# Copies of bank A ahead of norm and halves in the steps of a block pair; the norm by two chunks; weight work spread over four places

## The chip, the cores and the metric

One core of one Trainium2 chip. The metric is the device time of the whole program in microseconds (us). TensorE (PE) multiplies, PEld are its weight loads; ScalarE is ACT, VectorE is DVE, GpSimd is POOL, and SyncE, SP, issues most transfers.

## The reference, cut to what matters

```python
kv = np.einsum('bhsd,bhse->bhde', k, v)           # 8 batches, 8 heads, 576 tokens, 64 per head
out = np.einsum('bhsd,bhde->bhse', q, kv)
rms = np.sqrt(np.mean(out * out, axis=-1, keepdims=True) + 1e-06)
x = out / rms * g_norm                            # then to 4608 tokens x 512
gate = 1.0 / (1.0 + np.exp(-(x @ w_gate)))        # w_gate, w_val: 512 x 1536
x = gate * (x @ w_val) @ w_out                    # w_out: 1536 x 512
h = x @ w_in                                      # 512 x 2048
g = np.where(h >= 1, h, np.where(h <= -1, 0.0, (h + 1) ** 2 / 4))
return g @ w_out2                                 # 2048 x 512
```

## The kernel before, in words

The 4608 tokens are nine blocks of 512, transposed: rows are channels, columns tokens. A number in fp32 is kept as two fp32r halves (`split`: ScalarE copies the high half, VectorE subtracts for the low one), and a product of two such numbers is three matmuls. Blocks 0 and 1 run first while the weights arrive, then blocks 2, 3 and 4 one at a time: for each of twelve slices f of the hidden layer 24 matmuls for gate and value, then `down`, 12 matmuls that add the slice's share to four accumulator banks. Blocks 5 and 6 are the first block pair, blocks 7 and 8 the second and last. After them class `Second` computes the second layer for all blocks; it is not touched.

A pair takes gate and value of two blocks together by a scheme of seven products (names a11, a12, a22, s1, s2, s3, s4; L648, six matmuls each) in place of eight. Bank A collects a11, then s2, s1 and s4 on top of it; between them ScalarE must copy it away: to bank D (pD), to u2, to u4, and at last through the sigmoid gate2. Bank A is one buffer, so each of these stands in front of the next product on A. D gives the sigmoid `gate`. Product a22 of a step is done by `finish` in the next step, and there VectorE completes `u2`, whose halves (gh, gl) are what `down` multiplies. Bank F, the attention's X, the norm's sums SS and kvps take turns in two more banks.

Beside the steps runs other work, put at places by hand: `at(n)` in `Pair.step` calls what the plan holds for step f and place n, and `work(dve, act)` goes on with the second layer's weights (decode, sums, halves, stores), so many pieces of VectorE and ScalarE. While the first pair runs, the attention and the norm of blocks 7 and 8 are made, eight chunks of 128 channels; blocks 2 to 4 carry the norm of the blocks behind them in the same way, with places 0, 1 and 2. A chunk's norm: its square, the halves of the square, a sum over each head by matmuls with ones (SS), the mean m, a reciprocal root r (an ACT function whose table must be loaded, as the sigmoid's must be after it), one Newton step t, and two products on VectorE. `manual_schedule` leaves every engine's instructions in the order of the code.

In the last pair the down weights wo are streamed ahead (`stream(n)`: until n sets of two tiles are held), from a pool of twelve tiles that the halves of the second layer's weights (w2half) use too; a half waits for the landing of the store that used its tile before.

Of the kernel before, what the change touches and what calls it, by code (L numbers as in the profile page):

```python
# [11 lines left out]
ALU = mybir.AluOpType  # L12
# [21 lines left out]
def attn_gated_mlp_kernel(ctx: ExitStack, tc: tile.TileContext, a: dict, out: bass.AP):  # L34
# [170 lines left out]
    def norm_stage(j, p, n):  # L205

        if n == 0:
            if p % 2 == 0:
                attn_two(j, p // 2)
                for i in range(2):  # L210
                    if p == 0:
                        load_q(j, 2 + i)
                    elif j >= J0 and not is_second(j):
                        load_q(j + 1, i)
                for c in range(p, p + 2):
                    x_of(j)[c] = x_tile(j, c)
                    act_copy(x_of(j)[c], xps.pop((j, c)))
            sq = state[j, p] = temp("sq", "sq")
            nc.scalar.activation(out=sq, in_=x_of(j)[p], func=AF.Square)
        elif n == 1:  # L220
            state[j, p] = split(state[j, p], half_tile(tp, "sqh", "sqh"), half_tile(tp, "sql", "sql"))
        elif n == 2:
            SS = at_tile("SS")
            for i in range(2):
                nc.tensor.matmul(SS, ones, state[j, p][i], start=i == 0, stop=i == 1)  # L225
            m = state[j, p] = temp("m", "nm")
            nc.scalar.activation(out=m, in_=SS, func=AF.Copy, scale=1.0 / D, bias=EPS)
        elif n == 3:
            m, r, t = state[j, p], temp("r", "nr"), temp("t", "nt")
            nc.scalar.activation(out=r, in_=m, func=AF.Abs_reciprocal_sqrt)  # L230
            nc.scalar.activation(out=t, in_=r, func=AF.Square)
            nc.vector.tensor_tensor(out=t, in0=t, in1=m, op=ALU.mult)
            state[j, p] = r, t
        else:
            r, t = state.pop((j, p))
            x = x_of(j)[p]
            nc.scalar.activation(out=t, in_=t, func=AF.Copy, scale=-0.5, bias=1.5)
            nc.vector.scalar_tensor_tensor(out=x, in0=x, scalar=gn, in1=r, op0=ALU.mult, op1=ALU.mult)
            nc.vector.tensor_tensor(out=x, in0=x, in1=t, op=ALU.mult)

    def norm_plan(chunks, every):

        plan = {}
        for i, (j, p) in enumerate(chunks):
            f = every * i
            for n, place in enumerate(((f, 2), (f + 1, 0), (f + 1, 1), (f + 1, 2), (f + 2, 1))):
                plan.setdefault(place, []).append((j, p, n))
        for place in plan.values():
            place.sort(key=lambda x: x[2] if x[2] else 9)
        return plan  # L250
# [349 lines left out]
    class Pair:  # L600
# [66 lines left out]
        def step(self, side, j, f, at, more):  # L667
# [16 lines left out]
            if f:  # L684
                split_g(j, f - 1, self.finish(f - 1))
            else:
                F = bank(side, 2, "pF")
                self.product(F, f, "s3")
            at(0)
            self.product(A, f, "s2", False)  # L690
            u2 = saved(A, "u2", "wol", 2)
            at(1)
            work(*portion)
            self.product(D, f, "a12", False)
            gate = sigmoid(D, "gate")
            at(2)
            work(*portion)
            self.product(A, f, "s1", False)
            u4 = saved(A, "u4", "sig", 1)
            if f:  # L700
# [3 lines left out]
            at(3)  # L704
# [5 lines left out]
            if f == F1 - 1:  # L710
                split_g(j + 1, 0, self.g2[0])
            if f:
                down(j, f - 1)
            self.pending = F, u2, gate
            work(3, 0)
# [301 lines left out]
    with tc.manual_schedule():  # L1017
# [294 lines left out]
        chunks = lambda *js: [(j, p) for j in js for p in range(NP)]  # L1312
# [11 lines left out]
        for j in range(2, J0):  # L1324
            tail = j == J0 - 1
            plan = norm_plan(chunks(j + 1, j + 2), 1) if tail else norm_plan(chunks(j + 1), 2)

            def at(f, n):
                for which in plan.get((f, n), ()):
                    norm_stage(*which)  # L1330
# [178 lines left out]
```

## Time and profile before

| | us |
|---|---|
| median of 3 runs | 1690.81 (1690.69 to 1692.56) |
| the profiled execution | 1693.95 |
| its span | 1692.0 |
| TensorE busy, of the span | 1650.2 (98%) |
| weight loads | 1375.3 (81%) |
| VectorE busy | 1133.7 (67%) |
| ScalarE busy | 913.7 (54%) |
| GpSimd busy | 186.5 (11%) |

The shares are of the whole span. Its stages: blocks 0 and 1 to about 245 us, blocks 2 to 4 to 573, the first pair's steps to 770, the rest of that pair's `down` to 807, the second pair's steps to 958, the rest of its `down` to 998, the second layer to the end. The busy time of TensorE contains matmuls at a lower clock; the granted clock stands beside it in the windows.

### The profile page before, as it was taken

The numbers are of one execution on the slowest core, as the hardware profiler recorded it, in microseconds if no ns is written. First come the engines' busy times: TensorE is split into PE (matmuls) and PEld (weight loads), VectorE is DVE, ScalarE is ACT, GpSimd is POOL, SyncE is SP. The second block draws the span as 40 slices with busy tenths as digits, with TensorE's granted clock in tenths as the row PEclk, the third lists the DMA queues.
The fourth block names the chain that finished last, engine by engine and source line by source line (L and its number), as shares of the span: only waits on it lengthen the run. The fifth ranks groups of instructions, "written<-read, shape, count | busy, mean of one in ns | idle before, by whom it ended". The sixth has DMA issues, their size and how long they took to land.

```text
span 1692.0 us, 22526 instructions
## 1 busy us (share of the span) xinstructions
PE 1650.2 (98%) x8132; PEld 1375.3 (81%) x8132; DVE 1133.7 (67%) x1682; ACT 913.7 (54%) x1366; POOL 186.5 (11%) x292
## 2 busy tenths in 40 slices
PE   8999999999999988889999999999999999999999
PEld 6778888888877766668787778888888888999998
DVE  5888846768845755447456655894697579569476
ACT  4444445546558646544343446754664675575573
POOL 1122132332301110110211200000000000000000
PEclk8999999999999998889999999999999999999999
DMA  9676785678768575656896577556755856687855
GB/s 290 240 243 227 246 289 191 212 235 269 236 199 267 177 264 170 214 190 248 307 338 239 174 275 274 203 199 245 234 193 186 299 175 220 245 296 258 315 183 193
DMA packets 134479, 400.05 MB, mean 236 GB/s; under 512 B 16856, under 2 KB 24152, under 8 KB 120288
## 3 DMA queue, kind: packets, MB, share of 16 engines
q1 hardware_dynamic: 113440, 331.48, 58.9%
q0 software_dynamic: 20928, 67.13, 10.6%
q8 instruction: 65, 1.06, 0.3%
q14 instruction: 46, 0.38, 0.1%
HBM read 315.18 MB, written 83.36 MB: 236 GB/s over the span
## 4 chain that ended last, share of the span: by engine, by line
PE 77%; issue 13%; POOL 3%; ACT 3%; DVE 2%; DMA 2%; SPq 0%; POOLq 0%; DVEq 0%; ACTq 0%
PE bank L798 20%; PE bank L958 20%; PE pA L648 6%; PE acc L94 4%; PE acc L96 4%; PE acc L95 4%; PE h L94 4%; PE h L95 4%; PE h L96 4%; PE pF L648 3%; POOL w1d L535 1%; PE kvps L159 1%; PE X L186 1%; PE pD L648 1%; PE SS L225 1%
## 5 line engine op out<-in xcount | busy, mean ns | idle before, releaser
L958 PE MATMUL bank<-gh,wo 128*128 128x512 f32 (+1 forms) x1680 | 345.8, 367 | 0.0
L958 PEld LDWEIGHTS bank<-gh,wo 128*128 128x128 f32 x1680 | 305.7, 188 | 39.3
L69 ACT ACTIVATE gh<-g 128x1024 fp32r<-128x1024 f32 (+2 forms) x164 | 151.0, 924 | 129.6 <-PE bank L958 99.3
L798 PE MATMUL bank<-x_t,wst 128*128 128x512 f32 (+1 forms) x960 | 210.0, 367 | 0.0
L798 PEld LDWEIGHTS bank<-x_t,wst 128*128 128x128 f32 x960 | 175.1, 188 | 22.5
L648 PE MATMUL pA<-xc,wc 128*128 128x512 f32 x576 | 156.2, 408 | 29.6 <-ACT u L69 28.3
L733 DVE TENSOR_TENSOR gh<-g,gh 128x1024 fp32r<-128x1024 f32 (+1 forms) x140 | 155.9, 1114 | 29.7 <-ACT gh L69 29.4
L94 PE MATMUL acc<-gh,woh 128*128 128x512 f32 x420 | 164.9, 393 | 0.0
L95 PE MATMUL acc<-gl,woh 128*128 128x512 f32 x420 | 164.2, 391 | 0.1
L798 PE MATMUL bank<-x_b,wst 128*128 128x512 f32 (+1 forms) x720 | 160.8, 367 | 0.0
L648 PEld LDWEIGHTS pA<-xc,wc 128*128 128x128 f32 x576 | 109.2, 194 | 63.5 <-ACT u L69 39.3
L69 ACT ACTIVATE kept<-bank 128x512 f32<-128x512 f32 (+1 forms) x200 | 109.3, 549 | 95.2 <-PE bank L798 82.0
L733 DVE TENSOR_TENSOR g<-bank,kept 128x512 f32<-128x512 f32 (+1 forms) x160 | 98.1, 634 | 84.4 <-ACT kept L69 45.8
L94 PE MATMUL h<-xh,w 128*128 128x512 f32 x384 | 151.6, 395 | 0.0
L95 PE MATMUL h<-xl,w 128*128 128x512 f32 x384 | 149.8, 390 | 0.2 <-DVE xl L84 0.2
L96 PE MATMUL h<-xh,w 128*128 128x512 f32 x384 | 149.5, 389 | 0.0
L798 PEld LDWEIGHTS bank<-x_b,wst 128*128 128x128 f32 x720 | 131.5, 188 | 16.9
L96 PE MATMUL acc<-gh,woh 128*128 128x512 f32 x324 | 126.8, 391 | 1.5 <-DMA woh<-wo1d 1.5
L848 DVE SCALAR_TENSOR_TENSOR g<-r,g 128x1024 f32<-128x1024 f32 (+1 forms) x70 | 78.0, 1115 | 73.1 <-ACT r L845 73.1
L842 ACT ACTIVATE r<-g,half 128x1024 f32<-128x1024 f32 (+1 forms) x70 | 74.4, 1063 | 65.3 <-DVE g L733 65.3
L95 PEld LDWEIGHTS acc<-gl,woh 128*128 128x128 f32 x420 | 79.1, 188 | 17.2 <-DVE gl L77 0.9
L94 PEld LDWEIGHTS acc<-gh,woh 128*128 128x128 f32 x420 | 79.1, 188 | 17.2 <-issue 0.4
(191 smaller groups left out, 2573.3 us busy)
## 6 DMA issues: line engine op xcount, KB each, us to landing
wo<-wo2d SPq DMA_DIRECT2D x70, 1024.0 KB, 4.9
wc<-w1d SPq DMA_DIRECT2D x168, 256.0 KB, 5.0
woh<-wo1d SPq DMA_DIRECT2D x162, 256.0 KB, 4.9
wst<-w2d SPq DMA_DIRECT2D x40, 1024.0 KB, 5.1
wst<-w2d SPq DMA_DIRECT2D x40, 768.0 KB, 4.6
raw<-in_w SPq DMA_DIRECT2D x32, 512.0 KB, 5.3
raw<-in_w_gv SPq DMA_DIRECT2D x24, 512.0 KB, 5.7
w1d<-w2half POOLq DMA_DIRECT2D x48, 256.0 KB, 3.6
```

The costliest lines, as they stand in the source:

```text
L69: nc.scalar.activation(out=o, in_=i, func=AF.Copy)
L94: nc.tensor.matmul(ps, w[0][:, wsl], x[0], start=first, stop=False)
L95: nc.tensor.matmul(ps, w[0][:, wsl], x[1], start=False, stop=False)
L96: nc.tensor.matmul(ps, w[1][:, wsl], x[0], start=False, stop=last)
L159: nc.tensor.matmul(ps[g * D:(g + 1) * D, e], k[:, s], v[:, s], start=c == 0, stop=c == NSC)
L186: nc.tensor.matmul(X[g][e * D:(e + 1) * D, t0:t1], kvw[b % NKV][s, i, e], q[e][s, t0:t1], start=True, stop=True)
L648: nc.tensor.matmul(o, w[:, h, sl], x[c][l], start=first and c == n == 0, stop=c == 1 and n == 2, skip_group_check=True)
L733: nc.vector.tensor_tensor(out=o, in0=x, in1=y, op=op)
L798: nc.tensor.matmul(bank, self.ws[w][h][:, sl], self.xo[x][:, l, c], start=first and c == n == 0, stop=c == 1 and n == 2, skip_group_check= ...
L842: nc.scalar.activation(out=r, in_=v, func=AF.Relu, bias=self.half, scale=0.5)
L848: nc.vector.scalar_tensor_tensor(out=v, in0=r, scalar=1.0, in1=v, op0=ALU.min, op1=ALU.max)
L958: nc.tensor.matmul(bank[i][o], self.wo2[2 * i + k // 2][:, k % 2 * 2 + e, h, o * P:(o + 1) * P], ops[m][:, l, e], start=first, stop=k == H ...
```

## The change

In `Pair.step` the copy u2 is issued before the halves of the former step's result (`split_g`), u4 before the sigmoid `gate`, and `work` is called at places 1, 2 and 3 and at the end, where it takes a ScalarE piece too. Place 3 now lies behind s4 and gate2. The norm is planned by units of two chunks in eight stages: attention and the X copies, square, halves, sums, both roots side by side, both squares of the roots, the rest. The second chunk's mean, root and t take the buffers of square and halves (tags sq, sqh, sql). In the last pair at most three sets of wo are held from step 7 on, where there were five, and `finish` of the last step comes before the second layer's first loads.

```diff
--- before.py
+++ after.py
@@ -202,51 +202,71 @@
         nc.vector.tensor_tensor(out=lo, in0=sq, in1=hi.bitcast(F32), op=ALU.subtract)
         state[j, p] = hi, lo
 
-    def norm_stage(j, p, n):
-
-        if n == 0:
-            if p % 2 == 0:
-                attn_two(j, p // 2)
-                for i in range(2):
-                    if p == 0:
-                        load_q(j, 2 + i)
-                    elif j >= J0 and not is_second(j):
-                        load_q(j + 1, i)
-                for c in range(p, p + 2):
-                    x_of(j)[c] = x_tile(j, c)
-                    act_copy(x_of(j)[c], xps.pop((j, c)))
+    def norm_stage(j, i, n):
+
+        ps = 2 * i, 2 * i + 1
+        tags = ("nm", "nr", "nt"), ("sq", "sqh", "sql")
+
+        def square(p):
             sq = state[j, p] = temp("sq", "sq")
             nc.scalar.activation(out=sq, in_=x_of(j)[p], func=AF.Square)
+
+        def halves(p):
+            state[j, p] = split(state[j, p], half_tile(tp, "sqh", "sqh"), half_tile(tp, "sql", "sql"))
+
+        def mean(e):
+            SS = at_tile("SS")
+            for h in range(2):
+                nc.tensor.matmul(SS, ones, state[j, ps[e]][h], start=h == 0, stop=h == 1)
+            m = state[j, ps[e]] = temp("m", tags[e][0])
+            nc.scalar.activation(out=m, in_=SS, func=AF.Copy, scale=1.0 / D, bias=EPS)
+
+        if n == 0:
+            attn_two(j, i)
+            for e in range(2):
+                if i == 0:
+                    load_q(j, 2 + e)
+                elif j >= J0 and not is_second(j):
+                    load_q(j + 1, e)
+            for p in ps:
+                x_of(j)[p] = x_tile(j, p)
+                act_copy(x_of(j)[p], xps.pop((j, p)))
         elif n == 1:
-            state[j, p] = split(state[j, p], half_tile(tp, "sqh", "sqh"), half_tile(tp, "sql", "sql"))
+            square(ps[0])
         elif n == 2:
-            SS = at_tile("SS")
-            for i in range(2):
-                nc.tensor.matmul(SS, ones, state[j, p][i], start=i == 0, stop=i == 1)
-            m = state[j, p] = temp("m", "nm")
-            nc.scalar.activation(out=m, in_=SS, func=AF.Copy, scale=1.0 / D, bias=EPS)
+            halves(ps[0])
+            square(ps[1])
         elif n == 3:
-            m, r, t = state[j, p], temp("r", "nr"), temp("t", "nt")
-            nc.scalar.activation(out=r, in_=m, func=AF.Abs_reciprocal_sqrt)
-            nc.scalar.activation(out=t, in_=r, func=AF.Square)
-            nc.vector.tensor_tensor(out=t, in0=t, in1=m, op=ALU.mult)
-            state[j, p] = r, t
+            mean(0)
+            halves(ps[1])
+        elif n == 4:
+            mean(1)
+        elif n == 5:
+            for e, p in enumerate(ps):
+                m, r = state[j, p], temp("r", tags[e][1])
+                nc.scalar.activation(out=r, in_=m, func=AF.Abs_reciprocal_sqrt)
+                state[j, p] = m, r
+        elif n == 6:
+            for e, p in enumerate(ps):
+                m, r = state[j, p]
+                t = temp("t", tags[e][2])
+                nc.scalar.activation(out=t, in_=r, func=AF.Square)
+                nc.vector.tensor_tensor(out=t, in0=t, in1=m, op=ALU.mult)
+                state[j, p] = r, t
         else:
-            r, t = state.pop((j, p))
-            x = x_of(j)[p]
-            nc.scalar.activation(out=t, in_=t, func=AF.Copy, scale=-0.5, bias=1.5)
-            nc.vector.scalar_tensor_tensor(out=x, in0=x, scalar=gn, in1=r, op0=ALU.mult, op1=ALU.mult)
-            nc.vector.tensor_tensor(out=x, in0=x, in1=t, op=ALU.mult)
-
-    def norm_plan(chunks, every):
+            for p in ps:
+                r, t = state.pop((j, p))
+                x = x_of(j)[p]
+                nc.scalar.activation(out=t, in_=t, func=AF.Copy, scale=-0.5, bias=1.5)
+                nc.vector.scalar_tensor_tensor(out=x, in0=x, scalar=gn, in1=r, op0=ALU.mult, op1=ALU.mult)
+                nc.vector.tensor_tensor(out=x, in0=x, in1=t, op=ALU.mult)
+
+    def norm_plan(units, begin, places):
 
         plan = {}
-        for i, (j, p) in enumerate(chunks):
-            f = every * i
-            for n, place in enumerate(((f, 2), (f + 1, 0), (f + 1, 1), (f + 1, 2), (f + 2, 1))):
-                plan.setdefault(place, []).append((j, p, n))
-        for place in plan.values():
-            place.sort(key=lambda x: x[2] if x[2] else 9)
+        for k, unit in enumerate(units):
+            for n, (f, place) in enumerate(places):
+                plan.setdefault((begin(k) + f, place), []).append((norm_stage, *unit, n))
         return plan
 
     def inv_rms(SS, m, r):
...
@@ -682,26 +702,26 @@
             self.product(A, f, "a11")
             act_copy(D, A)
             if f:
-                split_g(j, f - 1, self.finish(f - 1))
+                g = self.finish(f - 1)
             else:
                 F = bank(side, 2, "pF")
                 self.product(F, f, "s3")
             at(0)
             self.product(A, f, "s2", False)
             u2 = saved(A, "u2", "wol", 2)
+            if f:
+                split_g(j, f - 1, g)
             at(1)
             work(*portion)
             self.product(D, f, "a12", False)
-            gate = sigmoid(D, "gate")
-            at(2)
-            work(*portion)
             self.product(A, f, "s1", False)
             u4 = saved(A, "u4", "sig", 1)
+            gate = sigmoid(D, "gate")
             if f:
                 F = bank(side, 2, "pF")
                 self.product(F, f, "s3")
             tt(u4, F, u4, ALU.add)
-            at(3)
+            at(2)
             work(*portion)
             self.product(A, f, "s4", False)
             gate2 = sigmoid(A, "gate2")
@@ -709,10 +729,12 @@
             tt(g2, gate2, u4, ALU.mult)
             if f == F1 - 1:
                 split_g(j + 1, 0, self.g2[0])
+            at(3)
+            work(*portion)
             if f:
                 down(j, f - 1)
             self.pending = F, u2, gate
-            work(3, 0)
+            work(3, 1)
 
 
     class Second:
...
@@ -1323,11 +1345,13 @@
 
         for j in range(2, J0):
             tail = j == J0 - 1
-            plan = norm_plan(chunks(j + 1, j + 2), 1) if tail else norm_plan(chunks(j + 1), 2)
+            every = 2 if tail else 4
+            places = (0, 2), (0, 2), (1, 0), (1, 1), (1, 2), (2, 0), (2, 1), (2, 2)
+            plan = norm_plan(units(j + 1, j + 2) if tail else units(j + 1), lambda k: every * k, places)
 
             def at(f, n):
                 for which in plan.get((f, n), ()):
-                    norm_stage(*which)
+                    which[0](*which[1:])
 
             norm_tags = ("nm", "nr", "nt", "sq")
             for f in range(F1):
...
@@ -1391,17 +1415,14 @@
             pair.g2 = {}
             plan = {}
             if more:
-                for i, (u, p) in enumerate(chunks(j + 2, j + 3)):
-                    for n, place in enumerate(((i + 1, 1), (i + 2, 0), (i + 2, 3), (i + 3, 0), (i + 3, 2))):
-                        plan.setdefault(place, []).append((norm_stage, u, p, n))
-                for place in plan.values():
-                    place.sort(key=lambda x: x[3])
+                places = (0, 1), (0, 2), (0, 3), (1, 0), (1, 2), (1, 3), (2, 0), (2, 2)
+                plan = norm_plan(units(j + 2, j + 3), lambda k: 2 * k + 1, places)
                 for u in range(2):
                     b = ((j + 3 + u) * T - 1) // S
                     if b > kv_done[0]:
                         kv_done[0] = b
                         for i in range(2):
-                            plan.setdefault((4 * u + 2 * i, 3), []).insert(0, (kv_product, b, i))
+                            plan.setdefault((4 * u + 2 * i, 2), []).insert(0, (kv_product, b, i))
                             for p in range(2 * i, 2 * i + 2):
                                 plan.setdefault((4 * u + i - 1, 3), []).append((load_kv, b, p))
 
...
@@ -1417,15 +1438,15 @@
                     n = f + F1 - 7
                     kept_wo[n] = stream_wo(n, [half_tile(tp, "wok", t, bufs=2 if t == "qraw" else 1) for t in LAST[n]])
                     wos.pop(n)
-                stream(2 if f < 7 else 4 if more else 5)
+                stream(2 if f < 7 else 4 if more else 3)
                 pair.step(side, j, f, at, more)
             acc_side[0] = side
             stream(4)
+            g = pair.finish(F1 - 1)
             if not more:
                 combos.close()
                 second = Second()
                 second.begin()
-            g = pair.finish(F1 - 1)
             down(j + 1, 0)
             split_g(j, F1 - 1, g)
             split_g(j + 1, 1, pair.g2[1])
```

What this moves on ScalarE in step 5 of the first pair, behind pD and gh (before; u_6573 is u2, u_6617 is u4):

```order
L69 ACTIVATE sqh<-sq 128x512
L230 ACT_TABLE_LOAD
L230 ACTIVATE r<-m 128x512
L231 ACTIVATE t<-r 128x512
L69 ACTIVATE u_6573<-pA 128x512
L69 ACTIVATE xn<-X 128x512 x2
L219 ACTIVATE sq<-xn 128x512
L476 ACTIVATE dt<-raw 128x512
L672 ACT_TABLE_LOAD
L672 ACTIVATE gate<-pD 128x512
L237 ACTIVATE t<-t 128x512
L69 ACTIVATE u_6617<-pA 128x512
```

The same step of the change, from the copy pD on (u_6589 is u2, u_6630 is u4):

```order
L69 ACTIVATE pD<-pA 128x512
L253 ACTIVATE t<-r 128x512 x2
L69 ACTIVATE u_6589<-pA 128x512
L69 ACTIVATE gh<-u_6465 128x512
L69 ACTIVATE xn<-X 128x512 x2
L69 ACTIVATE w2half<-dt 128x256
L69 ACTIVATE u_6630<-pA 128x512
L692 ACT_TABLE_LOAD
L692 ACTIVATE gate<-pD 128x512
L260 ACTIVATE t<-t 128x512 x2
L212 ACTIVATE sq<-xn 128x512
L69 ACTIVATE w2half<-dt 128x512
```

Before, a half of the square, a table load, a root and its square stand ahead of u2, and a table load and a sigmoid ahead of u4. Now two squares stand ahead of u2; gh, the X copies and one weight half stand between u2 and u4, and the one table load of the step follows u4. In the whole program ACT_TABLE_LOAD stands 52 times before and 28 times in the change.

ScalarE at the boundary of steps 5 and 6, from the sigmoid gate2 on, before (u_6713 is u2 of step 6):

```order
L672 ACTIVATE gate_6646<-pA 128x512
L69 ACTIVATE pD<-pA 128x512
L69 ACTIVATE gh<-u_6573 128x512
L69 ACTIVATE sqh<-sq 128x512
L230 ACT_TABLE_LOAD
L230 ACTIVATE r<-m 128x512
L231 ACTIVATE t<-r 128x512
L69 ACTIVATE u_6713<-pA 128x512
```

and in the change (u_6747 is u2 of step 6):

```order
L692 ACTIVATE gate_6667<-pA 128x512
L69 ACTIVATE sqh<-sq 128x512
L212 ACTIVATE sq<-xn 128x512
L69 ACTIVATE w2half<-su 128x512 x2
L69 ACTIVATE pD<-pA 128x512
L222 ACTIVATE m<-SS 128x512
L69 ACTIVATE sqh<-sq 128x512
L69 ACTIVATE u_6747<-pA 128x512
```

The half of the square that stood ahead of u2 now stands behind gate2, with the second chunk's square and two weight halves, and all of these are ahead of the next step's pD; behind pD come a mean and the second half.

In block 2, ScalarE from the X copies of block 3's second two chunks to a root, before:

```order
L69 ACTIVATE xn<-X 128x512 x2
L219 ACTIVATE sq<-xn 128x512
L69 ACTIVATE sqh<-sq 128x512
L69 ACTIVATE w2half<-su 128x512
L567 ACTIVATE sig<-h_3183 128x512
L227 ACTIVATE m<-SS 128x512
L69 ACTIVATE gh<-gf 128x512
L69 ACTIVATE w2half<-su 128x512
L230 ACT_TABLE_LOAD
L230 ACTIVATE r<-m 128x512
L231 ACTIVATE t<-r 128x512
```

and in the change:

```order
L69 ACTIVATE xn<-X 128x512 x2
L212 ACTIVATE sq<-xn 128x512
L69 ACTIVATE sqh<-sq 128x512
L212 ACTIVATE sq<-xn 128x512
L69 ACTIVATE w2half<-su 128x512
L587 ACTIVATE sig<-h_3185 128x512
L222 ACTIVATE m<-SS 128x512
L69 ACTIVATE sqh<-sq 128x512
L69 ACTIVATE gh<-gf 128x512
L69 ACTIVATE w2half<-su 128x512
L222 ACTIVATE m<-SS 128x512
L247 ACT_TABLE_LOAD
```

Before, a chunk has its square, its sum and its root in one go, and the next one begins two steps later. Now both chunks' squares stand together, and the second mean, which follows the second sum, stands three rows behind the half of its square.

## Rows read from the trace of the kernel before

**Rows 1.** Windows: us, busy us (instructions) by engine, TensorE's clock, DMA share, GB/s
```profile
245.00:573.00 328.00, 328.00 (x1732) 266.21 (x1731) 225.22 (x397) 200.55 (x314) 74.11 (x108) 1.00 0.69 225
573.30:770.05 196.75, 171.20 (x776) 132.54 (x775) 102.52 (x172) 105.01 (x170) 23.61 (x36) 0.93 0.61 200
595.00:613.00 18.00, 17.14 (x109) 13.70 (x108) 11.38 (x21) 6.14 (x11) 0.73 (x1) 1.00 0.96 340
807.00:958.10 151.10, 146.62 (x632) 117.05 (x631) 86.53 (x150) 57.37 (x104) 29.06 (x44) 1.00 0.75 261
```

**Rows 2.** Waits of TensorE, 573 to 770 us: total, times, longest
```profile
PE pA L648 <- ACT u L69: 24.5, 11, 3.1
PE pA L648 <- ACT gate L672: 0.7, 1, 0.7
```

**Rows 3.** Timeline of TensorE, step 3: start, us, instruction [idle before]
```profile
612.96 1.52 PE L648 MATMUL pA<-xc,wc 128*128 128x512 f32 x6
614.32 1.52 PE L648 MATMUL pF<-xc,wc 128*128 128x512 f32 x6
...
617.13 1.10 PE L186 MATMUL X<-qraw,kvw 64*64 64x448 f32 x16
618.16 1.66 PE L648 MATMUL pD<-xc,wc 128*128 128x512 f32 x6
621.63 1.67 PE L648 MATMUL pA<-xc,wc 128*128 128x512 f32 x6 [1.80 <-ACT u L69]
...
626.86 1.66 PE L648 MATMUL pA<-xc,wc 128*128 128x512 f32 x6 [1.75 <-ACT u L69]
...
631.08 1.30 PE L648 MATMUL pA<-xc,wc 128*128 128x512 f32 x5
```

**Rows 4.** Timeline of ScalarE in the same step
```profile
614.58 0.58 ACT L69 ACTIVATE pD<-pA 128x512 f32<-128x512 f32 x1 [3.55 <-PE pA L648]
617.34 0.63 ACT L69 ACTIVATE gh<-u 128x512 fp32r<-128x512 f32 x1 [2.17 <-DVE u L664]
...
618.50 1.28 ACT L230 ACT_TABLE_LOAD   x1
619.80 0.63 ACT L230 ACTIVATE r<-m 128x512 f32<-128x512 f32 x1
...
620.99 0.58 ACT L69 ACTIVATE u<-pA 128x512 f32<-128x512 f32 x1
...
623.60 1.28 ACT L672 ACT_TABLE_LOAD   x1
...
626.22 0.59 ACT L69 ACTIVATE u<-pA 128x512 f32<-128x512 f32 x1
```

**Rows 5.** The chain that ended last, step 0: start, us
```profile
580.26 1.32 PE kvps L159 x40
```

**Rows 6.** Groups by line, ScalarE: busy us, mean ns, idle before
```profile
L230 ACT ACT_TABLE_LOAD x24 | 30.8, 1283 | 0.4
```

**Rows 7.** Timeline of VectorE in the same step 3
```profile
615.88 0.69 DVE L663 TENSOR_TENSOR u<-pF,u 128x512 f32<-128x512 f32 x1 [3.00 <-PE pF L648]
...
624.23 0.75 DVE L238 SCALAR_TENSOR_TENSOR xn<-xn,gn,r 128x512 f32<-128x512 f32 x1
```

**Rows 8.** Timeline of TensorE, a step of the second pair
```profile
871.09 1.52 PE L648 MATMUL pD<-xc,wc 128*128 128x512 f32 x6
872.55 1.65 PE L648 MATMUL pA<-xc,wc 128*128 128x512 f32 x6
874.04 1.52 PE L648 MATMUL pF<-xc,wc 128*128 128x512 f32 x6
```

**Rows 9.** Waits of TensorE, 770 to 960 us
```profile
PE pA L648 <- ACT u L69: 3.8, 3, 1.7
```

**Rows 10.** Waits of ScalarE, 807 to 960 us
```profile
ACT w2half L69 <- DMA w2d<-w2half: 4.8, 2, 2.6
```

**Rows 11.** Waits, 955 us to the end
```profile
PE acc L96 <- DMA woh<-wo1d: 1.5, 3, 0.5
```

More of the change, by code (lines that the diff above doesn't have):

```diff
@@ L1311, in attn_gated_mlp_kernel @@
         pair = Pair()
-        chunks = lambda *js: [(j, p) for j in js for p in range(NP)]
+        units = lambda *js: [(j, i) for j in js for i in range(NP // 2)]
         LAST = {F1 - 3: ("sq", "zeros"), F1 - 2: ("sqh", "sql"), F1 - 1: ("qraw", "qraw")}
```

## Prediction

> **What bounds the kernel now.** I read the stages by windows first. TensorE is the bound: in blocks 2 to 4 it is busy for all 328.0 us of the stretch [rows 1]. The exception is the first block pair: 171.2 us busy in 196.75 us at a granted clock of 0.93, where the second pair takes 151.1 us at 1.00. Then the waits of that stretch: TensorE waits 24.5 us in 11 waits for ScalarE's `u` (the copies u2 and u4 of bank A) and 0.7 us for a sigmoid [rows 2]. Then the timeline of one step on the three engines, which says why.
>
> A step is seven products of six matmuls, 1.36 us each (612.96 to 614.32), and a `down` of 12 matmuls, 2.72 us at the same spacing of 0.227 us; 12.24 us in all. The step shown lasts from 612.96 to 631.08, 18.12 us [rows 3]. Product s1 starts at 621.63, 1.80 us late, because copy u2 runs at 620.99 only; ScalarE had first done gh, a half of the norm, a table load of 1.28 us, and two activations of the norm [rows 4]. Product s4 is 1.75 us late for the same reason: u4 ran at 626.22, behind a second table load, a sigmoid and weight work.
>
> **The first pair, summed.** The work of TensorE at the spacing of 0.227 us: 83 products x 1.36 = 112.9; 11 `down` x 2.72 = 29.9; four X products of 1.03 (617.13 to 618.16) = 4.1; eight norm sums of two matmuls = 3.6; two kvps of 1.32 [rows 5] = 2.6. That is 153.1 us, so the stretch holds 43.6 us too much. 25.6 are recorded waits (24.5, 0.7 and a small one); some 18 are left: 0.07 of the clock over 196.75 us is 13.8, and the rest is lost slots of about 0.2 us at many waits.
>
> What the change does there: over two steps ScalarE loads four tables now and two after (the two roots stand side by side, 24 loads fewer in the program, each 1.283 us [rows 6]); u2 is first in the queue behind the copy pD and the norm's piece at that place; u4 stands ahead of the sigmoid and its table load. I walk a pair of steps of the changed order with the durations of one step [rows 3, 4, 7], from the start of a11 as zero. ScalarE starts 1.62 us after a product's start (612.96 to 614.58), its ops follow at about 0.55 us, VectorE's take 0.69 and 0.75.
>
> Odd step (attention is made in it): pD 1.62 to 2.20; two squares to 3.3; s2 at 2.72, so u2 4.34 to 4.92; X to 5.11, a12 to 6.47; s1 is due at 6.47 and its wait is gone by 1.5 us. gh, two xn copies and one half of weight work end near 7.1; s1's end lets u4 run 8.09 to 8.67; s4 is due at 9.19: no wait. Table load and sigmoid to 10.55; two norm ops, a square, a weight half; gate2 at 12.8 to 13.4. The next a11 is due at 13.27 and needs bank A: 0.15 us of wait. This is what is late next. VectorE meanwhile: u4's sum from 9.4, four norm products, a weight half, g2, then the low half of the square at 14.35 to 15.04. Even step: ScalarE's second square needs that buffer, 15.1 to 15.7, two weight ops, and only then pD, 16.8 to 17.4. s2 is due at 13.4 + 2.72 + 0.45 = 16.6: 0.8 us of wait. The rest of the even step has u2 and u4 0.5 us ahead of need, and the load for the roots lies beside `down`. So a wait of about 1.0 us in two steps, where the step shown alone had 3.55.
>
> Four such pairs cost 4.0. Step 0 has no `down`, and step 1 waits for its sigmoid as now: 0.7. For halves of weights that wait for the landing of a store, which the second pair shows, I allow 1.5, and 2.5 for lost slots: 153.1 + 8.7 = 161.8, which is 35 us less. That counts on the clock at 1.00, 2.4 GHz. It is 1.00 in the first pair's own steps 1 and 2 (595 to 613 us), which hold 0.9 us without work, and through the second pair, whose longest wait is 1.7 us [rows 1, 9]; the changed steps are of that kind.
>
> The Trainium skill ("ScalarE: Activation LUTs", section "What ACT_TABLE_LOAD costs") states that a switch of tables costs the load of about 1283 ns and a drain of about 1380 ns. The load agrees with the trace; the drain doesn't, since the root starts at 619.80, 0.02 us behind the load's end [rows 4]. With the page's price gate2 of the odd step would come 1.38 us later, four times, and the sum would end at about 1657 us; I go by the row.
>
> **The second pair.** It has no norm. Its work is 112.9 + 29.9 = 142.8 of 151.1 us. Product s1 comes 1.46 us after the one before, not 1.36, and the one after it 1.49: gh stands ahead of u2 there too, 0.23 us in each of 11 steps, 2.5 us [rows 8]. 3.8 us are waits for `u` [rows 9], all but 0.7 because a weight half waited up to 2.6 us for a store's landing with u4 behind it [rows 10]. In the new order u2 is ahead of gh and one weight half, not two, stands ahead of u4. What is left: 1.4 at step 0, 1.0 for stores, 1.3 for the rest: 146.5, 4.5 us less.
>
> **The other edits.** Weight work moves by places, not in amount; more ScalarE pieces per step end it before the last step. It costs nothing while the queues have the slack walked above; with that cover gone one piece is 0.6 us per step, 13 us over both pairs. The load-ahead of wo in the last pair falls from five to three: TensorE waits 1.5 us for woh after it [rows 11]. Three sets leave six of the twelve buffers to the weight halves. Bounds: 1.5 us gained, or one set of two transfers late, about 2 us lost; I take 0. `finish` before the second layer's first loads: these wait for that product anyway; 0. X and the loads of q that go with it stay in the step and at the place where they were. The SP queue keeps its transfers; loads of raw weights change places with neighbours, and a load on SP has two steps of lead.
>
> Blocks 2 to 4 have no idle time to win. There the new order puts the second chunk's sum one `down` behind the first's, not two steps. Its low half goes into the buffer that the first sum still reads: first sum 0 to 0.45 and read to 0.6, its mean to 1.25, copy of the square to 1.9, low half to 2.6; the second sum is due at 0.45 + 2.72 = 3.17. Slack 0.55 us, eight units. Bounds: nothing, or three ops of weight work on VectorE ahead of it (2.1 us), 1.5 us of wait each, 12 us. The nearer row is VectorE's 225.2 us of 328.0: I take 0.5 us in all.
>
> **Sum.** -35 - 4.5 + 0 + 0.5 = -39 us. The profiled execution took 1693.95 us with a span of 1692.0; it becomes 1653 and 1655. The median of the runs shown is 3.1 us below that execution, 1690.81: 1652 us.
>
> **Rivals.**
> 1. The clock doesn't come back. For it: waits of 0.8 us stay at the start of every second step, and the lower clock began only after steps with waits. Against: the stretch from 595 to 613 us [rows 1] runs at 1.00 with as much idle time. 0.07 of 162 us is 11 us: about 1664 us.
> 2. The sums of blocks 2 to 4 wait. For it the slack of 0.55; against, VectorE is idle for a third of that stretch. With 12 us: 1664 us.
> 3. The wait only changes its name: ScalarE's queue is held in the odd steps by the square that needs VectorE, and pD is late by what u2 and u4 were. For it: in the walk this wait is already the largest. Against: VectorE would have to be 3 us later in each. Then hardly anything is gained but the table loads: 1680 to 1691 us.
> 4. Slower. The mechanism is stores: near the end of an odd step two weight halves stand ahead of pD, one ahead of gate2 and one ahead of u4. If each waits 2.6 us for a landing, as the longest did, these four cost 10.4 us in two steps, 41.6 over four pairs, more than the 39 won: 1694 us. It decides from 9.8 us in two steps on. Against: the first pair shows no wait for a store on ScalarE at all, and it moves less per us than the second (200 against 261 GB/s) [rows 1]; at the new pace that is 200 x 196.75 / 161.8 = 243.
>
> **Numbers.** Forecast 0.76, by itself 1645 to 1662 us: the lower end is the pair of steps without any wait and a gain at woh, the upper twice the walked waits and 2 us at woh. Rivals 1 and 2: 0.09 and 0.06. Rival 3: 0.05. Rival 4: 0.04. The range 1645 to 1668 takes in rivals 1 and 2, and leaves the last two out with a part of the edges. 0.2%, 3.4 us, is about what a measurement here can tell from no change. Faster: 0.76 + 0.09 + 0.06 and 0.02 of rival 3, 0.93; no change: the other 0.03 of rival 3; slower: 0.04.
>
> **What would show it.** Right: no wait of s1 for `u` in the first pair, steps of 13 to 14 us, clock 1.00, 28 table loads; TensorE's largest waits there are for pD and gate2, under 1.2 us each. Wrong: waits for `u` above 5 us, a clock below 0.97 in that stretch, a wait of SS before 573 us, or woh waits above 3 us.

## The result, and the profile after

The change takes 1650.61 us (median of 4 runs, 1649.93 to 1650.98) against 1690.91 us of the kernel before in the same rounds: a ratio of 0.9759 [0.9742, 0.9776], 40.3 us less. The forecast was 39 us less and a time of 1652. A second measurement (below, beside the kernel before in its own rounds) gave 0.9759 again. The profiled execution took 1650.7 us with a span of 1648.6.

| stage, us | before | forecast | after |
|---|---|---|---|
| blocks 0 to 4 | 573.3 | 573.8 | 573.0 |
| first pair's steps | 196.6 | 161.8 | 160.2 |
| rest of its `down` | 37.1 | 37.1 | 37.8 |
| second pair's steps | 151.1 | 146.5 | 144.8 |
| from there to the end | 733.9 | 733.9 | 732.9 |

The windows of the change (length, busy us and count of PE, PEld, DVE, ACT, POOL, then TensorE's clock), which answer to [rows 1]: blocks 2 to 4, the first pair's steps, the second's.

```profile
245.00:573.00 328.00, 328.00 (x1732) 266.22 (x1731) 224.32 (x397) 177.72 (x298) 74.18 (x108) 1.00 0.69 226
573.30:733.00 159.70, 155.63 (x774) 123.75 (x773) 108.18 (x185) 97.04 (x168) 29.20 (x44) 1.00 0.77 263
771.00:915.80 144.80, 143.43 (x632) 118.12 (x631) 79.52 (x137) 54.98 (x101) 28.22 (x43) 1.00 0.74 262
```

Blocks 2 to 4 are full as before. The first pair is now busy for all but 4 us, at a granted clock of 1.00 (2.4 GHz) instead of 0.93. What TensorE still waits for there answers to [rows 2]:

```profile
PE pA L668 <- ACT pD L69: 3.0, 4, 1.0
PE pA L668 <- ACT gate L692: 0.7, 1, 0.7
PE SS L220 <- DVE kvw L72: 0.4, 1, 0.4
```

No wait for `u` is left of 24.5 us. Three of the four waits for pD (0.67 to 1.00 us, in steps 4, 6 and 8) are those that the walk had; step 2, where it had one too, has none, and the fourth, of 0.61 us in step 10, has another cause, shown below. The timeline of TensorE in a pair of steps (start, us, instruction, idle before it), the odd one from 612.31 on, which answers to [rows 3]:

```profile
612.31 1.52 PE L668 MATMUL pA<-xc,wc 128*128 128x512 f32 x6
613.67 1.52 PE L668 MATMUL pF<-xc,wc 128*128 128x512 f32 x6
615.03 1.52 PE L668 MATMUL pA<-xc,wc 128*128 128x512 f32 x6
616.48 1.10 PE L186 MATMUL X<-qraw,kvw 64*64 64x448 f32 x16
617.50 1.66 PE L668 MATMUL pD<-xc,wc 128*128 128x512 f32 x6
619.00 1.54 PE L668 MATMUL pA<-xc,wc 128*128 128x512 f32 x6
620.38 1.52 PE L668 MATMUL pF<-xc,wc 128*128 128x512 f32 x6
621.74 1.52 PE L668 MATMUL pA<-xc,wc 128*128 128x512 f32 x6
...
625.82 1.54 PE L668 MATMUL pA<-xc,wc 128*128 128x512 f32 x6
627.20 1.52 PE L668 MATMUL pF<-xc,wc 128*128 128x512 f32 x6
...
629.88 1.66 PE L668 MATMUL pA<-xc,wc 128*128 128x512 f32 x6 [0.70 <-ACT pD L69]
...
639.99 1.52 PE L668 MATMUL pA<-xc,wc 128*128 128x512 f32 x6
```

The odd step lasts 13.51 us (612.31 to 625.82) without a wait; s1 at 619.00 and s4 at 621.74, both 1.8 us late before, follow at once. The even one lasts 14.17 us (to 639.99), with a wait of 0.70 ahead of s2. ScalarE in the same steps, which answers to [rows 4]:

```profile
613.87 0.58 ACT L69 ACTIVATE pD<-pA 128x512 f32<-128x512 f32 x1 [0.50 <-PE pA L668]
614.36 1.14 ACT L253 ACTIVATE t<-r 128x512 f32<-128x512 f32 x2
616.59 0.60 ACT L69 ACTIVATE u<-pA 128x512 f32<-128x512 f32 x1 [1.08 <-PE pA L668]
617.08 0.62 ACT L69 ACTIVATE gh<-u 128x512 fp32r<-128x512 f32 x1
...
620.58 0.60 ACT L69 ACTIVATE u<-pA 128x512 f32<-128x512 f32 x1 [1.54 <-PE pA L668]
621.20 1.28 ACT L692 ACT_TABLE_LOAD   x1
...
627.63 0.63 ACT L212 ACTIVATE sq<-xn 128x512 f32<-128x512 f32 x1 [1.46 <-DVE sql L77]
628.17 0.62 ACT L69 ACTIVATE w2half<-su 128x512 fp32r<-128x512 f32 x1
628.69 0.65 ACT L496 ACTIVATE dt<-raw 128x512 f32<-128x512 f32 x1
629.25 0.58 ACT L69 ACTIVATE pD<-pA 128x512 f32<-128x512 f32 x1
...
638.08 1.28 ACT L247 ACT_TABLE_LOAD   x1
639.38 1.15 ACT L247 ACTIVATE r<-m 128x512 f32<-128x512 f32 x2
```

Both copies `u` now wait for TensorE (1.08 and 1.54 us), where TensorE waited for them, and the table load comes behind the second. Then the square that needs VectorE's half of the square (1.46 us), two pieces of weight work, and pD behind them at 629.25: the wait that the prediction called late next. Counted from the odd step's start, the square runs at 15.3 us and pD at 16.9, where the walk had 15.1 and 16.8.

The wait in step 10 comes by another way. There a weight half stands ahead of pD and waits 3.75 us for VectorE's piece `dt`:

```profile
710.33 0.42 ACT L69 ACTIVATE w2half<-dt 128x256 fp32r<-128x256 f32 x1 [3.75 <-DVE dt L506]
710.66 0.58 ACT L69 ACTIVATE pD<-pA 128x512 f32<-128x512 f32 x1
```

One thing that the prediction did not see stands in ScalarE's waits of the first pair before the change:

```profile
ACT gh L69 <- DVE u L664: 23.9, 11, 2.2
```

Copy gh needs the sum `u` of VectorE, and stood at the head of ScalarE's queue for some 2.2 us before it could run, eleven times, with the norm's half, the table load and the root behind it, and u2 behind those [rows 4]. The queue was late because its head waited, not because it had too much to do: ScalarE is busy for 105 of 197 us there. In the new order u2 stands in that place, which waits only for TensorE's own product.

### The profile page after: what moved, and what is told of

Its sections match the earlier page's. It is cut to its first block, busy times and chain, and to the rows that moved or that the text cites. A ratio compares the mean times of both kernels' runs of the same rounds, so it can differ in the third digit from the quotient of the medians.

```text
span 1648.6 us, 22517 instructions
## 1 busy us (share of the span) xinstructions
PE 1631.9 (99%) x8132; PEld 1368.0 (83%) x8132; DVE 1131.6 (69%) x1682; ACT 879.4 (53%) x1342; POOL 186.7 (11%) x292
## 4 chain that ended last, share of the span: by engine, by line
PE 93%; DMA 3%; DVE 2%; ACT 2%; issue 0%; SPq 0%; DVEq 0%; ACTq 0%
PE bank L820 21%; PE bank L980 21%; PE pA L668 7%; PE h L94 7%; PE h L95 6%; PE h L96 6%; PE acc L94 5%; PE acc L96 5%; PE acc L95 5%; PE pF L668 3%; PE pD L668 2%; DMA kv_early<-in_kv_main 1%; PE kvps L159 1%; PE X L186 1%; DMA woh<-wo1d 1%; PE SS L220 1%
## 5 line engine op out<-in xcount | busy, mean ns | idle before, releaser
L668 PE MATMUL pA<-xc,wc 128*128 128x512 f32 x576 | 147.4, 391 | 5.0 <-ACT pD L69 3.0
L820 PEld LDWEIGHTS bank<-x_b,wst 128*128 128x128 f32 x720 | 131.5, 188 | 16.9
```

The costliest lines, as they stand in the source:

```text
L668: nc.tensor.matmul(o, w[:, h, sl], x[c][l], start=first and c == n == 0, stop=c == 1 and n == 2, skip_group_check=True)
L820: nc.tensor.matmul(bank, self.ws[w][h][:, sl], self.xo[x][:, l, c], start=first and c == n == 0, stop=c == 1 and n == 2, skip_group_check= ...
```

## The experiments

The kernel before itself took 1690.91 to 1693.85 us in the four sets of rounds, 0.2% apart, so versions are compared by their ratio to it in the same rounds, and by the length of the first pair's steps ("first pair" below; 196.6 us before, 160.2 in the change). My theory was that the places of u2 and u4 in ScalarE's queue win the time. The rival was that fewer table loads win it: the norm by two chunks cuts them from 52 to 28.

**Only the new step, with the norm of before.**

```diff
 # in the kernel before: all of the hunk on Pair.step, for instance
-                split_g(j, f - 1, self.finish(f - 1))
+                g = self.finish(f - 1)
...
             u2 = saved(A, "u2", "wol", 2)
+            if f:
+                split_g(j, f - 1, g)
```

> The changed step of a block pair (copies u2 and u4 ahead, weight work at three places and the end), with the norm of before, chunk by chunk, 52 table loads. Theory 1, the gain of 40 us is the place of the copies: walked with the durations of before, an even step has sqh, a table load and two ops ahead of u2, which ends at 5.9 where s1 is due at 5.5, 0.5 us of wait; an odd step 0.25 us at s4; some 0.8 us in two steps, about as in the change: 1650 to 1657 us. Theory 2, the gain is the 24 table loads that are gone: they are all back, so 1675 to 1690 us.

Measured 1648.59 us, ratio 0.9742 [0.9728, 0.9757], first pair 158.4 us, with all 52 table loads. TensorE's waits there:

```profile
PE pA L648 <- ACT u L69: 1.8, 5, 0.7
PE SS L225 <- DVE kvw L72: 0.4, 1, 0.4
```

The step alone gives the whole gain. The new norm adds nothing to it, and in this stretch costs 1.8 us: the change records 4.1 us of waits there, most of them for pD, and this kernel 2.2. Between pD and u2 stands all that stood there before but gh, load and root among it; it runs in the time in which ScalarE used to wait with gh:

```profile
613.78 0.58 ACT L69 ACTIVATE pD<-pA 128x512 f32<-128x512 f32 x1 [3.04 <-PE pA L648]
614.27 0.62 ACT L69 ACTIVATE sqh<-sq 128x512 fp32r<-128x512 f32 x1
614.92 1.28 ACT L230 ACT_TABLE_LOAD   x1
616.21 0.63 ACT L230 ACTIVATE r<-m 128x512 f32<-128x512 f32 x1
616.87 0.63 ACT L231 ACTIVATE t<-r 128x512 f32<-128x512 f32 x1
617.41 0.58 ACT L69 ACTIVATE u<-pA 128x512 f32<-128x512 f32 x1
```

u2 starts 3.63 us behind pD here, and 6.41 before [rows 4]. The step's hunk also moves the weight work to other places; no run moves that work alone, so its own share of the gain is open.

**Only the new norm, with the step of before.** The edits of the end stay in.

```diff
 # in the change: the hunk on Pair.step taken back, for instance
             u2 = saved(A, "u2", "wol", 2)
-            if f:
-                split_g(j, f - 1, g)
```

> The step of before, the norm by two chunks with the roots side by side, 28 table loads. Theory 1: u2 stands behind gh, u4 behind place 2, a weight half and the sigmoid with its table load: about 1 us at s1 and 3.7 us at s4 of the odd steps, 1 us at s1 of the even ones; half of the old waits stay, part of the lower clock too: 1665 to 1675 us. Theory 2: the loads are gone, 1650 to 1657 us.

Measured 1662.05 us, ratio 0.9820 [0.9802, 0.9839], first pair 167.1: better than I expected. A timeline of ScalarE shows why the second edit, too, ends most of the wait:

```profile
616.35 0.58 ACT L69 ACTIVATE pD<-pA 128x512 f32<-128x512 f32 x1 [1.86 <-PE pA L668]
619.16 0.63 ACT L69 ACTIVATE gh<-u 128x512 fp32r<-128x512 f32 x1 [2.23 <-DVE u L684]
619.70 1.14 ACT L253 ACTIVATE t<-r 128x512 f32<-128x512 f32 x2
620.74 0.58 ACT L69 ACTIVATE u<-pA 128x512 f32<-128x512 f32 x1
```

The 2.23 us at gh are there, but no load follows: u2 comes 4.39 us behind pD. The long wait took gh's wait and the load together, and either edit breaks it. So the gains don't add: 43 us (step) and 30 us (norm), and 40 with both.

**The change, with u2 behind gh again.**

```diff
-                g = self.finish(f - 1)
+                split_g(j, f - 1, self.finish(f - 1))
...
-            if f:
-                split_g(j, f - 1, g)
             at(1)
```

> The change, only split_g (gh, gl) back ahead of place 0, s2 and u2. Theory 1: s1 waits 0.3 us in odd and 0.8 us in even steps of the first pair, 0.23 us in each step without norm (14 of them, as in the second pair before): 4.5 + 3, so 1656 to 1660 us. Theory 2: no change from 1650.6.

Measured 1664.44 us, ratio 0.9834 [0.9818, 0.9851], first pair 168.9; more than I expected. TensorE waits 6.3 us for `u`, seven times, and ScalarE 25.1 us with gh at the head of its queue. The second pair takes 147.5 instead of 144.8: 2.7 us, the 0.23 us a step that the prediction read there [rows 8].

**The change, with u4 behind the sigmoid and weight work again.**

```diff
             self.product(D, f, "a12", False)
+            gate = sigmoid(D, "gate")
+            at(2)
+            work(*portion)
             self.product(A, f, "s1", False)
             u4 = saved(A, "u4", "sig", 1)
-            gate = sigmoid(D, "gate")
...
-            at(2)
-            work(*portion)
```

> The change, only u4 back behind the sigmoid gate, place 2 and its weight work (place 2 ahead of s1 again). Theory 1: in odd steps the table load, the sigmoid, two norm ops, a square and a weight half stand ahead of u4, s4 waits 3 to 3.7 us, four times, 12 to 15 us, with some microseconds of lower clock and a few waits for stores in the second pair: 1664 to 1674 us. Theory 2: no change from 1650.6.

Measured 1655.07 us, ratio 0.9783 [0.976, 0.9805], first pair 163.3: a miss, u4's place costs much less, 3.1 us of the pair. TensorE waits 6.3 us for it, five times, but at most 1.7 us and not the 3 to 3.7 that I had expected: in the odd step from 641.74 on the table load starts at 648.51, as soon as the weight half ahead of it ends, and u4 runs 10.64 us behind the step's start. The waits for pD are gone; the second square, ahead of pD, waits for VectorE at most 0.8 us there and 2.1 in the change.

**Only u2 ahead of gh, and only u4 ahead of the sigmoid, each in the kernel before.**

```diff
 # first kernel
-                split_g(j, f - 1, self.finish(f - 1))
+                g = self.finish(f - 1)
...
             u2 = saved(A, "u2", "wol", 2)
+            if f:
+                split_g(j, f - 1, g)
...
 # second kernel
             self.product(D, f, "a12", False)
-            gate = sigmoid(D, "gate")
-            at(2)
-            work(*portion)
             self.product(A, f, "s1", False)
             u4 = saved(A, "u4", "sig", 1)
+            gate = sigmoid(D, "gate")
+            at(2)
+            work(*portion)
```

> The kernel before with one edit: u2 ahead of gh and gl (split_g). Theory 1: s1 waits 0 in odd and 0.5 us in even steps in place of 1.8 and 3.1; u4 still has a table load, the sigmoid, a norm op and weight work ahead of it, so s4 waits 2 to 3 us in every step; the waits of the first pair fall from 25.6 to some 20 us, the clock stays low: 1676 to 1684 us, of which 2.5 come from the second pair. A third theory, that the clock carries the cost (18 of the 43.6 us): no more than the waits' own 5 to 8 us are won while long waits remain.

> The kernel before with one edit: s1 and u4 ahead of the sigmoid gate, place 2 and its weight work. Theory 1: s1's waits of 1.8 and 3.1 us stay, s4's fall from 1.8 to 0.2: some 7 of the 24.5 us go, with a part of the lower clock, and the second pair loses its two waits for stores (3.1 us): 1670 to 1680 us.

u2 alone: 1668.06 us, ratio 0.9848 [0.9833, 0.9863], first pair 172.0. u4 alone: 1683.35 us, 0.9935 [0.992, 0.995], 189.2. Both missed, the first to the better, the second to the worse. The windows 640 to 680 us, first of u4 alone and then of u2 alone, and the waits of TensorE in the pair, in the same order:

```profile
640.00:680.00 40.00, 34.45 (x138) 26.60 (x139) 21.33 (x37) 25.60 (x42) 2.48 (x4) 0.91 0.50 158
```

```profile
640.00:680.00 40.00, 36.86 (x164) 27.81 (x164) 23.68 (x40) 25.89 (x42) 4.01 (x6) 1.00 0.65 216
```

```profile
PE pA L648 <- ACT u L69: 20.7, 9, 3.1
```

```profile
PE pA L648 <- ACT u L69: 12.3, 12, 1.9
```

With u4 alone the waits of s1 stay, up to 3.1 us, and the clock is 0.91 (0.87 in the same window of the kernel before). With u2 alone twelve waits of at most 1.9 us are left and the clock is 1.00. Below stand a product behind a long wait and the next one, in the run with u4 alone; the windows that hold them and the time after; and a product behind a shorter wait, with u2 alone:

```profile
640.67 2.75 PE L648 MATMUL pA<-xc,wc 128*128 128x512 f32 x6 [3.06 <-ACT u L69]
643.21 2.06 PE L648 MATMUL pF<-xc,wc 128*128 128x512 f32 x6
```

```profile
640.67:643.30 2.63, 2.63 (x7) 2.04 (x8) 1.54 (x3) 0.98 (x2) 1.16 (x2) 0.54 0.00 0
643.30:645.20 1.90, 1.90 (x8) 1.54 (x7) 0.00 (x0) 1.73 (x2) 0.21 (x1) 0.73 0.93 267
645.20:648.00 2.80, 2.80 (x14) 2.32 (x13) 1.45 (x4) 2.79 (x6) 0.00 (x0) 1.00 0.99 354
```

```profile
640.23 1.65 PE L648 MATMUL pA<-xc,wc 128*128 128x512 f32 x6 [1.55 <-ACT u L69]
```

Six matmuls take 2.75 us behind the 3.06 us wait, at a clock of 0.54, and 1.65 behind the 1.55; the next six take 2.06 instead of 1.52. So this wait cost another 1.6 us. The wait of s1, which u2's place ends, was worth most: of the 24.6 us that u2 alone wins in the pair, 12.2 are recorded waits (25.6 us before, 13.4 with u2 alone), and the rest is the clock and lost slots.

**The change, with the roots apart again.**

```diff
+        def root(e):
+            m, r = state[j, ps[e]], temp("r", tags[e][1])
+            nc.scalar.activation(out=r, in_=m, func=AF.Abs_reciprocal_sqrt)
+            state[j, ps[e]] = m, r
...
         elif n == 4:
+            root(0)
             mean(1)
         elif n == 5:
-            for e, p in enumerate(ps):
...
+            root(1)
```

> The change with the first chunk's root one place earlier, ahead of the sigmoid gate2, the second where it was: 36 table loads, eight more, all in the first pair and beside down in the even steps. Theory 1 (place of the copies): the loads lie behind u4, gate2 comes some 2.5 us later in the even steps, just in time for the next a11; 0 to 0.5 us in two steps, 1650 to 1653 us. Theory 2 (table loads): 8 x 1.28 = 10 us, 1659 to 1662 us.

Measured 1654.42 us, ratio 0.9765 [0.9749, 0.9781], first pair 162.6 with 36 loads. The ratio can't be told from the change's, and the pair is 2.4 us longer, or 0.3 per added load of 1.28 us. With u2 and u4 ahead of them, most of the time of table loads lies beside matmuls.

**The change, with the second square behind pD.** It is meant to take away the wait that the walk found.

```diff
         elif n == 2:
             halves(ps[0])
-            square(ps[1])
         elif n == 3:
+            square(ps[1])
             mean(0)
```

> The change with the second chunk's square moved from place 3 of the odd step to place 0 of the even step, behind the copy pD, so that it no longer waits for VectorE with pD behind it. The four waits of s2 for pD (3.0 us in the profile of the change) are that square's wait: they go, u2 of the even step is still 0.3 us ahead of need: 1646.5 to 1648.5 us. If pD is late for the weight halves ahead of it instead, the waits stay: 1650 to 1651 us.

Measured 1648.06 us, ratio 0.9731 [0.9716, 0.9745], first pair 157.0, 3.3 us less than the change. The three waits for pD that the square made are gone; the one of 0.6 us in step 10, behind a weight half, is left. In step 4 ScalarE is idle for 0.16 us until a11 ends, runs pD at once and the square after it:

```profile
630.27 0.58 ACT L69 ACTIVATE pD<-pA 128x512 f32<-128x512 f32 x1 [0.16 <-PE pA L668]
630.76 0.63 ACT L212 ACTIVATE sq<-xn 128x512 f32<-128x512 f32 x1
```

**Four on one chip: the change again; with the norm of before in blocks 2 to 4; the norm of before everywhere with the change's step and end; the second square behind pD with a load-ahead of five.**

```diff
 # second kernel, blocks 2 to 4: the functions of before, as norm_plan_old
-            plan = norm_plan(units(j + 1, j + 2) if tail else units(j + 1), lambda k: every * k, places)
+            plan = norm_plan_old(chunks(j + 1, j + 2), 1) if tail else norm_plan_old(chunks(j + 1), 2)
 # third kernel: the first experiment with the diff's last hunk
-                stream(2 if f < 7 else 4 if more else 5)
+                stream(2 if f < 7 else 4 if more else 3)
 # fourth kernel: the experiment before this one, and
-                stream(2 if f < 7 else 4 if more else 3)
+                stream(2 if f < 7 else 4 if more else 5)
```

> The change itself once more, as the measure for the other three on the same chip. Expected: its ratio to before again at 0.976, within 0.0015, and the waits for pD four times 0.7 to 1.0 us in the first pair.

> The change, with the norms of blocks 2 to 4 by the plan of before (chunk by chunk; 44 table loads instead of 28). My theory: TensorE waits for nothing in these blocks by either plan, so the two differ by under 1.5 us (same ratio as the change within 0.001). The rival, that table loads cost time wherever they stand: 16 more loads at 1.28 us each, up to 20 us slower than the change, 1671.

> The step of the change and its order at the end of the last pair (products finished before the second stage begins, load-ahead of 3), with the norm of before everywhere. Against the run with only the new step it tells what the end's edits are worth. My theory: nothing, the ratio stays at 0.974 within 0.0015, and the stretch from the last step to the end stays within 1 us of 732.5. The rival: the shorter load-ahead leaves one transfer late, a wait of 1.4 us for it, as the change shows.

> The best version that the runs point to: the change with the second square of a norm unit issued one place later (behind the copy pD) and the load-ahead of 5 kept in the last pair. Expected: the four waits for pD gone as in the run with that edit alone, 2 to 4 us less than the change on this chip, ratio 0.973 to 0.975; the wait of 1.4 us for the transfer of wo gone if the load-ahead made it, still there if the transfer is bound by when its buffer comes free.

| | us | ratio | first pair | last step to end |
|---|---|---|---|---|
| the change | 1652.28 | 0.9759 [0.9743, 0.9774] | 160.3 | 735.3 |
| old norm in blocks 2 to 4 | 1651.61 | 0.9750 [0.9736, 0.9765] | 160.3 | 733.1 |
| old norm, new step and end | 1650.05 | 0.9749 [0.9729, 0.9769] | 158.4 | 732.2 |
| square behind pD, load-ahead 5 | 1649.93 | 0.9743 [0.9728, 0.9759] | 157.0 | 732.8 |

The intervals overlap: the norm of blocks 2 to 4 and the edits of the end are worth nothing that these runs can tell. The stretch to the end varies by 2.4 us between the two profiles of the change itself, so smaller differences there say nothing. The wait of 1.4 us for woh is 1.1 with five sets ahead and 0.6 in the third kernel, which holds three: these runs show no dependence on the number of sets. What the number of sets does show is in the second pair: in all five profiled kernels that hold five sets ScalarE waits there for stores of weight halves, two to four times, up to 2.6 us, and in none of the nine profiles with three (the first experiment and the third kernel differ in the end's edits alone). With u2 and u4 ahead they cost at most 0.3 us: the second pair takes 145.1 us in the fourth kernel, and 144.8 in the first experiment and in the change. The fourth kernel has the shortest first pair, 3.3 us under the change, yet its whole time is not told apart from it. One reason shows in the profiles: its blocks 0 to 4 took 576.0 us, those of the change in the same rounds 572.5. Such a difference comes without any change of the code: the third kernel and the first experiment have the same code there, and took 576.2 and 573.3 us.

## Why the prediction was right

- **The first pair.** Forecast 161.8 us, measured 160.2. The mechanism held: the new step takes away the waits for `u`, and its parts taken back bring them again. What I credited together, fewer table loads and the new places, the runs tell apart: the step alone does it all (158.4 us), and the norm alone would have done three quarters. Of the step's 38.2 us u2's place alone wins 24.6 and u4's alone 7.4. The walk did not ask what each part would do alone, and it had not seen gh's own 2.2 us of wait, in which the loads found room.
- **The clock.** The step counted on 1.00 because the changed steps hold little idle time; it is 1.00 in all of the pair, where no wait over 1.0 us is left, and rival 1 falls. 7.1 us over the 153.1 of work are left, of which 4.1 are recorded waits; before, it was 43.5 with 25.6. So 21.5 us of the gain are waits and 15 are clock and lost slots.
- **What is late next.** Four waits for pD of 0.6 to 1.0 us, forecast four of 0.8. For three of them the cause, the second square, is shown by the run that moves it. The fourth is a weight half's, which the walk did not have, and step 2 has none; that the number came to four is luck. The wait for gate2, forecast 0.15, is not there. With 3.0 us in all, pD is not late by what u2 and u4 were, and rival 3 falls.
- **Allowances.** 1.5 and 1.0 us for stores of weight halves were not needed: in neither pair does ScalarE show such a wait (the second profile of the change has one, of 1.0 us, in a first pair of 160.3 us), and rival 4, which rested on them, falls. It does not fall by the argument that I gave against it: at the new pace the first pair moves 263 GB/s, not 243, as much as the second, since 40 stores of halves are issued in it instead of 32. The allowances are most of the 3.3 us by which the two pairs are shorter than forecast. Lost slots came to 3.0 us (forecast 2.5), the waits for pD to 3.0 (forecast 4.0 with gate2's).
- **Table loads.** After the change, too, a load lasts 1.28 us, and the root starts 0.02 us behind its end (638.08, 639.38). The Trainium skill ("ScalarE: Activation LUTs", section "What ACT_TABLE_LOAD costs") gives the load some 1283 ns and a drain of some 1380 ns besides. The trace agrees with the load and shows no drain. The run with the roots apart says nothing against the drain, since its loads lie off the path; the start of the root does.
- **The second pair.** 144.8 against 146.5: 1.0 by the stores and 0.7 by lost slots, of which 0.6 are left where I allowed 1.3. Waits are 1.4 us, at step 0, as forecast.
- **The other edits.** Blocks 2 to 4: no wait of TensorE, so rival 2 falls; 0.5 was forecast. The wait for woh: 1.4 us in one piece, where it was 1.5 in three [rows 11]. Missed: the `down` behind the pair waits 0.5 us for gh and gl and is 0.8 us longer. It is so in all kernels with the new step (37.8 to 37.9 us) and in none with the old one (37.1); nor does it go when u2's or u4's place is taken back. The traces point at the weight work that now stands at the end of a step: VectorE goes on with it without a pause until the sum `u` behind the last product on F, which starts 2.36 us behind that product's start (733.18), and 1.56 before (769.89). No run takes only that work back.

```profile
771.45 0.69 DVE L663 TENSOR_TENSOR u<-pF,u 128x512 f32<-128x512 f32 x1 [0.96 <-PE pF L648]
```

```profile
735.20 0.43 DVE L486 TENSOR_TENSOR su<-su,dt 128x256 f32<-128x256 f32 x1
735.54 0.68 DVE L683 TENSOR_TENSOR u<-pF,u 128x512 f32<-128x512 f32 x1
```

- **The range.** Its ends were set wider than their own terms: the sum less the pairs' walked waits and the gain at woh is 1646.5 us, not 1645, and with these waits doubled and 2 us at woh it is 1658, not 1662. The measured time lies inside either.

Not settled: what brings the lower clock. In the first pair every wait of 2.5 us and more was followed by it. Of the five waits of 1.8 to 2.0 us in the kernel before two were, too, and of the three of 1.8 us in the run with u4 alone one (its six matmuls took 2.25 us); of twelve of at most 1.9 us with u2 alone none was. No run held a wait's length and changed what lies around it.

## What to carry to other kernels

In an engine's in-order queue, look for an instruction that itself waits for another engine and stands ahead of the copy that frees the bound engine's bank: moving the copy ahead of it can win the wait and all that has piled up behind it (here u2's place alone won 24.6 of 196.6 us). Two edits that shorten one chain of delays need not add; ask what each does alone, from the moment at which the copy is due. Walk the new order on every queue up to the next late thing: here that walk found the wait that was largest afterwards, and with it the edit that removes it.

## What the runs showed of the hardware

- The ten waits of 2.5 to 3.1 us in TensorE's products (five in the first pair of the kernel before, five with u4 alone) were each followed by a stretch at the lower level of the clock. Behind the one shown the granted clock was 0.54 over 2.6 us and 0.73 over the next 1.9, then 1.00, and it cost 1.6 us beyond itself. Behind a wait of 2.16 us (u2 behind gh) the six matmuls took 1.66 us, as behind short waits.
- The start of the program varies: with the same code its first 100 us had a clock of 0.95 in the first experiment and 0.91 in the kernel with the norm of before and the change's step and end, and blocks 0 to 4 took 573.3 and 576.2 us. A stage's own length tells edits of 2 us apart where whole times don't: the first pair took 160.2, 160.3 and 160.3 us in three profiles with the same code there.
